# Attention with two MoE-like layers on one core: the first layer's chunks beside the attention go from two of 288 tokens a batch in every step to one of 512 in every second step

## The chip, the cores and the metric

The kernel runs on one core of one Trainium2 chip. The metric is the device time of one execution in microseconds (us): the median of the runs before is 996.87 us (three runs, 996.81 to 996.87). TensorE is called PE, VectorE DVE, ScalarE ACT, GpSimd POOL, SyncE SP, as in the profile.

## The reference: what is computed

Inputs are in fp32; q, k, v are (4 batches, 8 heads, 576 positions, 64), s is (4, 8, 576).

```python
scores = scale * np.matmul(q, k.transpose(0, 1, 3, 2))
cum = np.cumsum(np.maximum(s, 0.0), axis=-1)
bias = -(cum[:, :, :, None] - cum[:, :, None, :])
scores = np.where(causal, -1000000000.0, scores + np.minimum(bias, 0.0))
scores = scores - np.max(scores, axis=-1, keepdims=True)
attn = np.exp(scores)
attn = attn / (np.sum(attn, axis=-1, keepdims=True) + 1e-09)
x = np.matmul(attn, v)                      # then (4 * 576 tokens, 512)
h = x @ w_in;  x = np.maximum(0.01 * h, h) @ w_out                                   # layer 0
h = x @ w2_in; x = (np.maximum(h, 0) + np.log1p(np.exp(-np.abs(h)))) @ w2_out        # layer 1
```

Both layers have 2304 tokens, 512 channels and 2048 hidden channels. The weights come in as double precision; the kernel splits each fp32 operand into a high and a low part, and takes three matmuls (high x high, high x low, low x high) for each product.

## The kernel before, in words

**The two stages.** Stage one is the attention, up to some 267 us; stage two is the rest of the two layers, in eight groups: layer 0 and 1, four groups of four blocks of 128 hidden channels each. The order of the instructions on every engine is the order in which the program records them (a manual schedule); a small clock (`later`, `tick`, L64 to L77) records a follow-up so many ticks later.

**The attention** (L154 to L467) takes two heads at a time, a pair p, 16 pairs in all. A pair has four steps, i = 0 to 3 (`order`, L419): the 512-wide last full block of rows, the 64 left-over rows of both heads (288 columns a piece), the 384-wide block, and the two first blocks together (256 + 128). Step n = 4p + i goes from 0 to 66, and has two ticks. Work on one step's tile goes through the engines over four steps. In step n, in this order, PE makes the scores of tile n+1 (L273, L283); DVE the minima of tile n (`maxima`, L302; for the left-over rows a last tiny combination, L307); ACT the exponentials of tile n (L316); DVE the divisors and POOL the normalisation of tile n-1 (L322, L323, L327); PE the transposes of tile n-2 into PSUM (L335, L339, L344), first half, then second half; ACT and DVE their copies to SBUF (L356, L358). In steps i = 0 and i = 2 PE ends with the product with V of the pair before (`pv`, L375), whose result ACT and DVE split into `xh` and `xl` (L382, L386).

**The fill units** (class `Fill`, L470 to L565). Between the first and the second transposes of each step, `fill.step(n)` (L491) puts in one unit of layer 0's first group (four hidden blocks) for a batch that is through the attention. An h unit (L530) is 12 matmuls for one hidden block; ACT, ACT again and POOL then make `gf`, `gh` and `gl` one tick after the other (L537, L542, L547). An o unit (L552) is 12 matmuls for one block of 128 output channels; ACT copies it to `o` (L562), and SP stores it to DRAM (`part`, L563). `ready(b)` (L519) lists the units of batch b once its last `xl` is there: two chunks of CW = S // 2 = 288 tokens, eight units each. `run` (L510) takes the first unit of the list if its weights and operands are recorded, else none. Weights are loaded and split by tables of steps (L480 to L482); the fourth output block is split in step 25, so that no o unit can be recorded ahead of step 28. Units that are left at the end are taken after the attention (L577).

**Stage two** starts with the first group for batch 3, as two chunks of 288 tokens (`first`, L596), then takes the other seven groups in five chunks (512, 512, 256, 512, 512). One step is one hidden block of one chunk: 12 matmuls of `h_mm` (L143), and three steps later the 12 matmuls of `out_mm` (L676). Partial sums of the fill units come back from `part` into `acc` by six loads (`load_acc`, L586, planned at L707).

**SBUF.** The split weights lie in `wpool` (L84), eight buffers for each of four tags, taken at the start.

Of the kernel before, what the change touches and what calls it, by code (L numbers as in the profile page):

```python
# [9 lines left out]
F32 = mybir.dt.float32  # L10
I32 = mybir.dt.int32
U32 = mybir.dt.uint32
F32R = mybir.dt.float32r
# [4 lines left out]
P = 128  # L18
NEG = -8.0e9
G = 4  # L20
# [10 lines left out]
def attn_moe_moe(ctx, tc, q, k, v, s, w1i, w1o, w2i, w2o, out):  # L31
    nc = tc.nc

    B, H, S = s.shape
    D = v.shape[-1]
    NT, DM = out.shape
    DFF = w1i.shape[1]
    KD = DM // P
    NF = DFF // P
    NG = NF // G  # L40
    NPAIR = H // 2
    NP = B * NPAIR
    NB = S // P
    TL = S - NB * P
    CW = S // 2
    scale = 1.0 / float(D) ** 0.5

    nc.scalar.preload_act_table_set("natural_log_exp_and_others")
# [1 line left out]
    def pool(name, bufs=1, **kw):  # L50
        return tc.tile_pool(name=name, bufs=bufs, **kw)

    dram = ctx.enter_context(pool("dram", space=bass.MemoryType.DRAM))
# [4 lines left out]
    xh = keep.tile([P, KD, NT], F32R, tag="xh", name="xh")  # L58
    xl = keep.tile([P, KD, NT], F32R, tag="xl", name="xl")
    bb_d = dram.tile([B * H, 2, S], F32R, tag="bb_d", name="bb_d")  # L60
    part = dram.tile([2 * B, P, KD, CW], F32, tag="part", name="part")


    todo = {}  # L64
# [2 lines left out]
    def later(n, fn, *args):  # L67
        todo.setdefault(clock[0] + n, []).append((fn, args))
# [12 lines left out]


    wt, wio = {}, {}
    wpool = ctx.enter_context(pool("wpool", bufs=2 * G))  # L84
    wio["tmp"] = ctx.enter_context(pool("wtmp", bufs=2))

    def load_w(layer, f, nm, place=None):
        w = ((w1i, w1o), (w2i, w2o))[layer]["io".index(nm)].bitcast(I32)
        raw = (place or wio[nm]).tile([P, 2 * DM], I32, tag="raw", name="raw" + nm)
        if nm == "i":  # L90
            nc.sync.dma_start(
                raw.rearrange("p (k f) -> p k f", k=KD),
                w[:, 2 * f * P:2 * (f + 1) * P].rearrange("(k p) f -> p k f", p=P),
            )
        else:
            nc.sync.dma_start(raw, w[f * P:(f + 1) * P, :])
        wt[layer, f, nm, "raw"] = raw.rearrange("p (e t) -> p e t", t=2)

    def split_w(layer, f, nm, at):

        raw = wt.pop((layer, f, nm, "raw"))
        L, Hw = raw[:, :, 0], raw[:, :, 1]
        m = wio["tmp"].tile([P, DM], I32, tag="wm", name="wm")
        t = wio["tmp"].tile([P, DM], I32, tag="wt", name="wt")
        nc.scalar.activation(m.bitcast(F32), Hw.bitcast(F32), AF.Abs)
        nc.scalar.activation(t, L.bitcast(U32), AF.Copy, scale=2.0 ** -29)

        mf = m.bitcast(F32)

        def clamp():  # L110
            nc.vector.tensor_scalar(mf, mf, D_MIN, D_MAX, op0=ALU.max, op1=ALU.min)

        def shift():
            nc.vector.tensor_scalar(m, m, 3, 0x3FFFFFFF, op0=ALU.logical_shift_left, op1=ALU.bitwise_and)

        def sign():
            nc.vector.scalar_tensor_tensor(m, Hw, -0x40000000, m, op0=ALU.bitwise_and, op1=ALU.bitwise_or)  # L117

        def add():
            nc.gpsimd.tensor_tensor(m, m, t, op=ALU.add)  # L120

        def high():
            hi = wpool.tile([P, DM], F32R, tag=f"w{nm}h", name=f"w{nm}h")
            nc.scalar.activation(hi, m.bitcast(F32), AF.Copy)
            wt[layer, f, nm] = [hi]

        def low():
            lo = wpool.tile([P, DM], F32R, tag=f"w{nm}l", name=f"w{nm}l")
            hi = wt[layer, f, nm][0]
            nc.gpsimd.tensor_tensor(lo, m.bitcast(F32), hi.bitcast(F32), op=ALU.subtract)  # L130
            wt[layer, f, nm].append(lo)

        for n, fn in zip(at, (clamp, shift, sign, add, high, low)):
            later(n, fn)


    def h_mm(ps, layer, f, xh, xl):
        hi, lo = wt[layer, f, "i"]
        n = 0
        for kk in range(KD):  # L140
            w = slice(kk * P, (kk + 1) * P)
            for a, b in ((hi[:, w], xh[:, kk, :]), (hi[:, w], xl[:, kk, :]), (lo[:, w], xh[:, kk, :])):
                nc.tensor.matmul(ps, a, b, start=n == 0, stop=n == 3 * KD - 1)  # L143
                n += 1
# [325 lines left out]
    class Fill:  # L470
# [20 lines left out]
        def step(self, n):  # L491
            if n == 4 * NPAIR + 1:
                self.begin()
            if n in self.loads:
                (f, nm), place = self.loads[n]
                load_w(0, f, nm, wio[place])
            if n in self.splits:
                split_w(0, *self.splits[n][0], (1, 2, 3, 4, 5, 6))
            self.run()

        def bank(self, nm):

            tag, bufs = ("m", 1) if not self.free else self.free.pop(0)
            if self.free is not None:
                self.free.append((tag, bufs))
            return self.ps.tile([P, 512], F32, tag=tag, name=nm, bufs=bufs)[:, :CW]

        free = None

# [7 lines left out]
                fn(*args)  # L517

        def ready(self, b):  # L519
            hs, os = [], []  # L520
            for ch in range(2):
                c0 = b * S + ch * CW
                x = xh[:, :, c0:c0 + CW], xl[:, :, c0:c0 + CW]
                gs = {}
                hs += [(self.h, (f, x, gs)) for f in range(G)]
                os += [(self.o, (dm, 2 * b + ch, gs)) for dm in range(KD)]

            self.units += hs[:G + 1] + os[:KD] + hs[G + 1:] + os[KD:]

        def h(self, f, x, gs):  # L530
            ps = self.bank("ps_h")
            h_mm(ps, 0, f, *x)
            new = lambda pool, nm, dt=F32: pool.tile([P, CW], dt, tag=nm, name=nm)

            def leaky():
                gf = new(self.tpool, "gf")
                nc.scalar.activation(gf, ps, AF.Prelu, alpha=0.01)  # L537
                later(1, high, gf)

            def high(gf):  # L540
                gh = new(self.gpool, "gh", F32R)
                nc.scalar.activation(gh, gf, AF.Copy)  # L542
                later(1, low, gf, gh)

            def low(gf, gh):
                gl = new(self.gpool, "gl", F32R)
                nc.gpsimd.tensor_tensor(gl, gf, gh.bitcast(F32), op=ALU.subtract)  # L547
                gs[f] = gh, gl

            later(1, leaky)  # L550

        def o(self, dm, c, gs):  # L552
            ps = self.bank("ps_o")
            w = slice(dm * P, (dm + 1) * P)
            for f in range(G):
                (wh, wl), (gh, gl) = wt[0, f, "o"], gs[f]
                for n, (a, b) in enumerate(((wh, gh), (wh, gl), (wl, gh))):
                    nc.tensor.matmul(ps, a[:, w], b, start=f == 0 and n == 0, stop=f == G - 1 and n == 2)  # L558

            def store():  # L560
                o = self.tpool.tile([P, CW], F32, tag="o", name="o")
                nc.scalar.activation(o, ps, AF.Copy)  # L562
                nc.sync.dma_start(part[c, :, dm, :], o)  # L563

            later(1, store)  # L565

    with pool("psA", bufs=2, space=PSUM) as psA:
# [11 lines left out]
            tick()  # L579
        fill.stack.close()  # L580

    for nm in "io":
        wio[nm] = ctx.enter_context(pool("raw" + nm))
    acc = ctx.enter_context(pool("accpool")).tile([P, KD, NT], F32, tag="acc", name="acc")

    def load_acc(c):  # L586
        nc.sync.dma_start(acc[:, :, c * CW:(c + 1) * CW], part[c])


    gpool = ctx.enter_context(pool("gpool", bufs=4, side="right"))  # L590
# [2 lines left out]
    ps_o = ctx.enter_context(pool("ps_o", bufs=5, space=PSUM))  # L593

    chunks = [(0, 512), (512, 512), (1024, NT - 2048), (NT - 1024, 512), (NT - 512, 512)]
    first = [((B - 1) * S + ch * CW, CW) for ch in range(2)]  # L596
    groups = [(layer, g) for layer in range(2) for g in range(NG)]
    steps = []
    for layer, g in groups:
# [17 lines left out]
    gs = {}  # L617
# [80 lines left out]
    for gi, (layer, g) in enumerate(groups[1:]):  # L698
        a, z = start[groups[gi]], start[layer, g]
        when = [(a + n - 1, a + n) for n in (0, 3, 6, 8, 11, 14, 16, 19)] if gi else [None] * 4 + [(0, 2), (1, 4), (3, 6), (5, 8)]  # L700
        for j, at in enumerate(when):
            if at:
                f, nm = divmod(j, 2)
                w = (layer, g * G + f, "io"[nm])
                plan.setdefault(at[0], []).append((load_w, w))
                plan.setdefault(at[1], []).append((split_w, (*w, (1, 1, 1, 1, 2, 2))))
    for c in range(2 * (B - 1)):  # L707
        plan.setdefault(2 * c + 2, []).append((load_acc, (c,)))

    for n, (layer, g, c, is_first, is_last, f) in enumerate(steps):  # L710
# [63 lines left out]
```

## Time and profile before

| | us |
|---|---|
| median of three runs | 996.87 |
| the profiled execution's own time | 996.93 |
| its span, first to last instruction | 995.1 |
| PE busy | 974.9 (98%) |
| POOL, ACT, DVE busy | 569.7, 539.3, 529.6 |

The profiled execution is 0.06 us above the median, and 1.8 us of its time lie outside the span. Busy shares are means over the whole span: the attention stage is read from its own stretches, by the chain of waits (what ended last, step by step) and by busy times in stretches of about one pair.

### The profile page before, as it was taken

The numbers are of one execution on the slowest core, as the hardware profiler recorded it, in microseconds if no ns is written. First come the engines' busy times: TensorE is split into PE (matmuls) and PEld (weight loads), VectorE is DVE, ScalarE is ACT, GpSimd is POOL, SyncE is SP. The second block draws the span as 40 slices with busy tenths as digits, with TensorE's granted clock in tenths as the row PEclk, the third lists the DMA queues.
The fourth block names the chain that finished last, engine by engine and source line by source line (L and its number), as shares of the span: only waits on it lengthen the run. The fifth ranks groups of instructions, "written<-read, shape, count | busy, mean of one in ns | idle before, by whom it ended". The sixth has DMA issues, their size and how long they took to land.

```text
span 995.1 us, 15228 instructions
## 1 busy us (share of the span) xinstructions
PE 974.9 (98%) x5498; PEld 810.7 (81%) x5498; DVE 529.6 (53%) x1139; ACT 539.3 (54%) x1153; POOL 569.7 (57%) x564
## 2 busy tenths in 40 slices
PE   7889999999999999999999999999999999999998
PEld 4567788888898888888888888888888888888886
DVE  7787556554222332132215447767687868763534
ACT  5777666666454333334334546676657655654452
POOL 6657455534256444444444446777867786775553
PEclk9999999999999999999999999999999999999999
DMA  5422333221153111111111111111111111100202
GB/s 176 140 84 80 104 112 115 64 74 44 37 197 128 43 43 43 43 43 43 45 41 43 43 42 43 43 43 43 43 43 43 43 42 43 43 1 1 85 22 85
DMA packets 38411, 62.04 MB, mean 62 GB/s; under 512 B 2790, under 2 KB 25830, under 8 KB 38336
## 3 DMA queue, kind: packets, MB, share of 16 engines
q1 hardware_dynamic: 38192, 60.74, 18.7%
q8 instruction: 44, 0.72, 0.3%
q10 hardware_dynamic: 144, 0.33, 0.1%
q14 instruction: 31, 0.25, 0.1%
HBM read 52.65 MB, written 8.40 MB: 61 GB/s over the span
## 4 chain that ended last, share of the span: by engine, by line
PE 92%; DVE 3%; ACT 3%; POOL 1%; issue 1%; ACTq 0%; POOLq 0%
PE ps_h L143 40%; PE ps_out L676 36%; PE pt_v L375 4%; PE pt_s L283 4%; PE ps_o L558 3%; PE pt_t L344 3%; PE pt_s L273 2%; ACT sc L316 1%; DVE sc L302 1%; PE pt_t L339 1%; DVE st L307 0%; ACT PA L356 0%; DVE wm L117 0%; ACT xh L382 0%; DVE acc L686 0%
## 5 line engine op out<-in xcount | busy, mean ns | idle before, releaser
L150 POOL TENSOR_TENSOR gl<-gf,gh 128x512 fp32r<-128x512 f32 (+2 forms) x148 | 181.2, 1225 | 138.6 <-ACT gh L149 128.9
L143 PE MATMUL ps_h<-xh,wih 128*128 128x512 f32 (+2 forms) x688 | 245.8, 357 | 0.6 <-ACT o L562 0.6
L143 PE MATMUL ps_h<-xl,wih 128*128 128x512 f32 (+2 forms) x688 | 243.8, 354 | 0.0
L143 PE MATMUL ps_h<-xh,wil 128*128 128x512 f32 (+2 forms) x688 | 243.7, 354 | 0.0
L686 DVE TENSOR_TENSOR acc<-ps_out,acc 128x512 f32<-128x512 f32 (+1 forms) x114 | 73.7, 662 | 164.4 <-PE ps_out L676 164.4
L641 POOL TENSOR_TENSOR t<-e,t 128x512 f32<-128x512 f32 (+1 forms) x80 | 112.4, 1405 | 72.0 <-DVE t L640 71.3
L327 POOL TENSOR_SCALAR sc<-sc,st 128x512 f32<-128x512 f32 (+4 forms) x160 | 87.6, 559 | 109.1 <-DVE st L323 65.5
L143 PEld LDWEIGHTS ps_h<-xh,wih 128*128 128x128 f32 x688 | 129.5, 188 | 19.1 <-ACT o L562 0.8
L143 PEld LDWEIGHTS ps_h<-xl,wih 128*128 128x128 f32 x688 | 129.6, 188 | 18.0
L143 PEld LDWEIGHTS ps_h<-xh,wil 128*128 128x128 f32 x688 | 129.5, 188 | 17.6
L625 ACT ACTIVATE gf<-ps_h 128x512 f32<-128x512 f32 (+2 forms) x68 | 36.6, 538 | 170.2 <-PE ps_h L143 170.0
L676 PE MATMUL ps_out<-woh,gl 128*128 128x512 f32 x288 | 112.3, 390 | 0.0
L676 PE MATMUL ps_out<-woh,gh 128*128 128x512 f32 x288 | 112.3, 390 | 0.0
L676 PE MATMUL ps_out<-wol,gh 128*128 128x512 f32 x288 | 112.2, 390 | 0.0
L149 ACT ACTIVATE gh<-gf 128x512 fp32r<-128x512 f32 (+2 forms) x148 | 85.4, 577 | 49.3 <-DVE gf L651 48.6
L316 ACT ACTIVATE sc<-sc,st 128x512 f32<-128x512 f32 (+2 forms) x144 | 83.5, 582 | 39.2 <-DVE st L307 19.7
L120 POOL TENSOR_TENSOR wm<-wm,wt 128x512 int32<-128x512 int32 x64 | 85.0, 1330 | 31.3 <-DVE wm L117 31.3
L302 DVE CUSTOM_DVE_ANT_0 sc<-pt_s,mask 128x512 f32<-128x512 f32 (+2 forms) x144 | 66.8, 480 | 59.5 <-PE pt_t L344 48.3
L676 PE MATMUL ps_out<-gh,wol 128*128 128x512 f32 (+2 forms) x272 | 97.8, 360 | 0.0
L676 PE MATMUL ps_out<-gh,woh 128*128 128x512 f32 (+2 forms) x272 | 97.7, 359 | 0.0
L676 PE MATMUL ps_out<-gl,woh 128*128 128x512 f32 (+2 forms) x272 | 97.7, 359 | 0.0
L640 DVE TENSOR_SCALAR t<-e 128x512 f32<-128x512 f32 (+1 forms) x80 | 44.3, 554 | 98.1 <-ACT e L631 98.1
(102 smaller groups left out, 1732.7 us busy)
## 6 DMA issues: line engine op xcount, KB each, us to landing
rawi<-in_moe_w_in SPq DMA_DIRECT2D x32, 512.0 KB
rawo<-in_moe_w_out SPq DMA_DIRECT2D x32, 512.0 KB
V<-in_v SPq DMA_DIRECT2D x16, 320.0 KB
Q<-in_q SPq DMA_DIRECT2D x15, 320.0 KB
K<-in_k SPq DMA_DIRECT2D x16, 288.0 KB
out<-acc SPq DMA_DIRECT2D x18, 256.0 KB
part<-o SPq DMA_DIRECT2D x24, 144.0 KB
acc<-part SPq DMA_DIRECT2D x6, 576.0 KB
```

What stands on the lines that cost most here:

```text
L120: nc.gpsimd.tensor_tensor(m, m, t, op=ALU.add)
L143: nc.tensor.matmul(ps, a, b, start=n == 0, stop=n == 3 * KD - 1)
L149: nc.scalar.activation(gh, gf, AF.Copy)
L150: nc.gpsimd.tensor_tensor(gl, gf, gh.bitcast(F32), op=ALU.subtract)
L283: nc.tensor.matmul(self.ps[j][:, c], x[r, t * P:(t + 1) * P], y[r, :(t + 1) * P], start=x is Q[i], stop=x is bq,)
L302: nc.vector.tensor_tensor_reduce(out=self.sc[:, j, c], in0=self.ps[j][:, c], in1=m, scale=-scale, scalar=3.0e38, op0=ALU.add, op1=ALU.min, ...
L316: nc.scalar.activation(x, x, AF.Exp, scale=-1.0, bias=self.stat(0, e), accum_out=self.stat(1, e))
L327: nc.gpsimd.tensor_scalar(x, x, self.stat(2, e), 1.0, op0=ALU.mult, op1=ALU.mult)
L640: nc.vector.tensor_scalar(t, e, 1.0, -1.0, op0=ALU.add, op1=ALU.add)
L641: nc.gpsimd.tensor_tensor(t, e, t, op=ALU.subtract)
L676: nc.tensor.matmul(ps, a, b, start=f == 0 and m == 0, stop=f == G - 1 and m == 2)
L686: nc.vector.tensor_tensor(d, o, d, op=ALU.add)
```

## The change

Layer 0's first group now takes one chunk of FW = 512 tokens for each of batches 0 to 2 beside the attention: tokens 0 to 511 with batch 0, 512 to 1023 with batch 1, 1024 to 1535 with batch 2. The other 768 tokens come first in stage two, as two chunks of 384. A fill unit is begun in even steps alone (i = 0 and i = 2), and in every step after 64. There are 24 units in place of 48. The weights' pool becomes one of six buffers, taken at the start, and one of two, taken after the attention; `part` comes back by three loads of 1 MB in place of six of 576 KB.

```diff
-    CW = S // 2
+    FW = 512
...
-    part = dram.tile([2 * B, P, KD, CW], F32, tag="part", name="part")
+    part = dram.tile([B - 1, P, KD, FW], F32, tag="part", name="part")
...
-    wpool = ctx.enter_context(pool("wpool", bufs=2 * G))
+    wpools = [ctx.enter_context(pool("wpool0", bufs=6))]
...
+        wp = wpools[(layer * NF + f) % (2 * G) // 6]
...
-            self.run()
+            if n % 2 == 0 or n > 4 * NP:
+                self.run()
...
         def ready(self, b):
-            hs, os = [], []
-            for ch in range(2):
-                c0 = b * S + ch * CW
-                x = xh[:, :, c0:c0 + CW], xl[:, :, c0:c0 + CW]
-                gs = {}
-                hs += [(self.h, (f, x, gs)) for f in range(G)]
-                os += [(self.o, (dm, 2 * b + ch, gs)) for dm in range(KD)]
-
-            self.units += hs[:G + 1] + os[:KD] + hs[G + 1:] + os[KD:]
+            c, gs = slice(b * FW, (b + 1) * FW), {}
+            x = xh[:, :, c], xl[:, :, c]
+            self.units += [(self.h, (f, x, gs)) for f in range(G)] + [(self.o, (dm, b, gs)) for dm in range(KD)]
...
+    wpools.append(ctx.enter_context(pool("wpool1", bufs=2)))
...
-        nc.sync.dma_start(acc[:, :, c * CW:(c + 1) * CW], part[c])
+        nc.sync.dma_start(acc[:, :, c * FW:(c + 1) * FW], part[c])
...
-    first = [((B - 1) * S + ch * CW, CW) for ch in range(2)]
+    n0 = (B - 1) * FW
+    n1 = (NT - n0) // 2
+    first = [(n0, n1), (n0 + n1, n1)]
...
-    for c in range(2 * (B - 1)):
+    for c in range(B - 1):
         plan.setdefault(2 * c + 2, []).append((load_acc, (c,)))
```

**POOL, between two pairs in the attention, h units in the list.** `sc` rows are normalisations (512 wide belongs to i = 0, 288 to i = 1, 384 to i = 2, 256 and 128 to i = 3), `gl` the last part of an h unit. Before:

```order
L547 TENSOR_TENSOR gl<-gf,gh 128x288
L327 TENSOR_SCALAR sc<-sc,st 128x512 x2
L547 TENSOR_TENSOR gl<-gf,gh 128x288
L327 TENSOR_SCALAR sc<-sc,st 128x288 x2
L547 TENSOR_TENSOR gl<-gf,gh 128x288
L327 TENSOR_SCALAR sc<-sc,st 128x384 x2
```

Now:

```order
L328 TENSOR_SCALAR sc<-sc,st 128x256
L328 TENSOR_SCALAR sc<-sc,st 128x128
L328 TENSOR_SCALAR sc<-sc,st 128x512 x2
L543 TENSOR_TENSOR gl<-gf,gh 128x512
L328 TENSOR_SCALAR sc<-sc,st 128x288 x2
L328 TENSOR_SCALAR sc<-sc,st 128x384 x2
L543 TENSOR_TENSOR gl<-gf,gh 128x512
```

A `gl` now stands behind the normalisations of two steps out of four, and is 512 wide.

**ACT, from the `xh` of step i = 0 to the `xh` of step i = 2.** `sc` are exponentials, PB and PA copies of transposes, `gf` and `gh` the parts of an h unit. Before:

```order
L382 ACTIVATE xh<-pt_v 128x192
L316 ACTIVATE sc,st<-sc,st 128x576
L356 ACTIVATE PB<-pt_t 128x3x128
L537 ACTIVATE gf<-ps_h 128x288
L316 ACTIVATE sc,st<-sc,st 128x384
L542 ACTIVATE gh<-gf 128x288
L316 ACTIVATE sc,st<-sc,st 128x384
L356 ACTIVATE PA<-pt_t 128x4x128
L537 ACTIVATE gf<-ps_h 128x288
L382 ACTIVATE xh<-pt_v 128x384
```

Now:

```order
L383 ACTIVATE xh<-pt_v 128x192
L538 ACTIVATE gh<-gf 128x512
L317 ACTIVATE sc,st<-sc,st 128x576
L357 ACTIVATE PB<-pt_t 128x3x128
L317 ACTIVATE sc,st<-sc,st 128x384 x2
L357 ACTIVATE PA<-pt_t 128x4x128
L533 ACTIVATE gf<-ps_h 128x512
L383 ACTIVATE xh<-pt_v 128x384
```

The `gh` of the even step's unit stands between `xh` and the left-over rows' exponential, and step i = 1 has no `gf` of its own.

**PE, the end of the attention.** `pt_t` are transposes, `pt_v` the last product with V. Before:

```order
L375 MATMUL pt_v<-PB,V_93 64x128 x2
L375 MATMUL pt_v<-PB,V_93 64x256 x4
L375 MATMUL pt_v<-PB,V_93 64x128 x2
L558 MATMUL ps_o<-gh,woh 128x288
L558 MATMUL ps_o<-gl,woh 128x288
L558 MATMUL ps_o<-gh,wol 128x288
```

Now:

```order
L345 MATMUL pt_t<-ident,sc 128x128 x6
L376 MATMUL pt_v<-PB,V_93 64x128 x2
L376 MATMUL pt_v<-PB,V_93 64x256 x4
L376 MATMUL pt_v<-PB,V_93 64x128 x2
L144 MATMUL ps_h<-xh,wih 128x384
L144 MATMUL ps_h<-xl,wih 128x384
```

No unit is left behind the last product with V; stage two's first matmul follows it at once.

## Rows read from the trace of the kernel before

**Rows 1.** The page: its span, and PE's busy time.
```profile
span 995.1 us, 15228 instructions
PE 974.9 (98%) x5498; PEld 810.7 (81%) x5498; DVE 529.6 (53%) x1139; ACT 539.3 (54%) x1153; POOL 569.7 (57%) x564
```

**Rows 2.** PE's waits from 270 us on: engine, line, releaser, total us, times, longest.
```profile
PE ps_h L143 <- ACT o L562: 0.6, 1, 0.6
```

**Rows 3.** Stretches of one pair: PE, PEld, DVE, ACT, POOL busy, granted clock, DMA.
```profile
28.20:41.20 13.00, 11.22 (x92) 7.86 (x92) 10.31 (x39) 9.52 (x28) 8.47 (x12) 1.00 0.35 116
...
117.80:135.00 17.20, 17.20 (x143) 14.33 (x141) 9.59 (x38) 11.84 (x33) 10.08 (x15) 1.00 0.29 96
```

**Rows 4.** The chain of waits in order of time, 117 to 137 us: start, us, what.
```profile
117.89 1.29 PE pt_s L283 x6
119.18 0.59 PE pt_t L339 x4
...
126.52 1.02 PE pt_s L283 x6
...
128.01 1.59 PE ps_h L143 x12
...
130.97 0.59 PE pt_t L344 x4
...
133.59 1.48 PE pt_v L375 x16
135.09 0.49 ACT xh L382
...
136.99 0.30 PE pt_t L335
```

**Rows 5.** The same view at five other places of stage one and stage two.
```profile
69.97 1.29 PE pt_s L283 x6
...
242.08 1.56 PE pt_v L375 x20
...
275.39 6.59 PE ps_h L143 x48
281.98 1.58 PE ps_out L676 x12
...
296.28 2.76 PE ps_h L143 x12
...
312.07 2.72 PE ps_out L676 x12
...
336.56 1.43 PE ps_h L143 x12
```

**Rows 6.** Instructions in order of time on POOL, DVE and ACT around 243 us.
```profile
243.18 1.36 POOL L327 TENSOR_SCALAR sc<-sc,st 128x512 f32<-128x512 f32 x2 [0.83 <-DVE st L323]
244.50 0.80 POOL L547 TENSOR_TENSOR gl<-gf,gh 128x288 fp32r<-128x288 f32 x1
...
243.92 0.43 ACT L542 ACTIVATE gh<-gf 128x288 fp32r<-128x288 f32 x1
245.35 0.78 ACT L316 ACTIVATE sc<-sc,st 128x576 f32<-128x576 f32 x1 [0.99 <-DVE st L307]
...
246.13 0.47 ACT L356 ACTIVATE PB<-pt_t 128x384 f32<-128x384 f32 x1
...
244.82 0.49 DVE L307 TENSOR_TENSOR st<-st 128x1 f32<-128x1 f32 x1
```

**Rows 7.** The same view at 79, 227 and 268 us, on POOL and DVE.
```profile
79.16 1.29 POOL L130 TENSOR_TENSOR wol<-wm,woh 128x512 fp32r<-128x512 f32 x1
...
79.75 0.71 DVE L307 TENSOR_TENSOR st<-st 128x1 f32<-128x1 f32 x1
...
227.72 0.16 DVE L307 TENSOR_TENSOR st<-st 128x1 f32<-128x1 f32 x1
...
268.29 0.56 DVE L386 TENSOR_TENSOR xl<-pt_v,xh 128x384 fp32r<-128x384 f32 x1 [4.62 <-ACT xh L382]
```

More of the change, by code (lines that the diff above doesn't have):

```diff
@@ L122, in high @@
         def high():
-            hi = wpool.tile([P, DM], F32R, tag=f"w{nm}h", name=f"w{nm}h")
+            hi = wp.tile([P, DM], F32R, tag=f"w{nm}h", name=f"w{nm}h")
             nc.scalar.activation(hi, m.bitcast(F32), AF.Copy)
@@ L127, in low @@
         def low():
-            lo = wpool.tile([P, DM], F32R, tag=f"w{nm}l", name=f"w{nm}l")
+            lo = wp.tile([P, DM], F32R, tag=f"w{nm}l", name=f"w{nm}l")
             hi = wt[layer, f, nm][0]
@@ L505, in bank @@
                 self.free.append((tag, bufs))
-            return self.ps.tile([P, 512], F32, tag=tag, name=nm, bufs=bufs)[:, :CW]
+            return self.ps.tile([P, 512], F32, tag=tag, name=nm, bufs=bufs)
         free = None
@@ L532, in h @@
             h_mm(ps, 0, f, *x)
-            new = lambda pool, nm, dt=F32: pool.tile([P, CW], dt, tag=nm, name=nm)
+            new = lambda pool, nm, dt=F32: pool.tile([P, FW], dt, tag=nm, name=nm)
             def leaky():
@@ L560, in store @@
             def store():
-                o = self.tpool.tile([P, CW], F32, tag="o", name="o")
+                o = self.tpool.tile([P, FW], F32, tag="o", name="o")
                 nc.scalar.activation(o, ps, AF.Copy)
```

## The prediction, made before the changed kernel ran

> **What bounds the kernel now.** First the page: PE is busy for 974.9 of 995.1 us [rows 1]. That is a mean over two unlike stages, so I looked next at PE's waits by stretch: from 270 us to the end PE waited 0.6 us in all [rows 2]. Stage two is therefore PE's own work, and a change there is worth what it does to the number and width of matmuls. For stage one I compared the busy times of two pairs [rows 3]. A pair without fill units took 13.00 us, with PE busy for 11.22 and no engine full: there the handing on from engine to engine sets the pace. A pair with four units took 17.20 us, and PE was busy for all of it. The chain of waits of that same pair is nearly all PE [rows 4]. So the units fill what the attention leaves of PE and then some, and with them stage one too is bound by PE. The granted clock is 1.00 in both stretches, so 2.4 GHz throughout, even where PE waited for 1.8 us in 13: I charge nothing for the clock.
>
> **Prices of PE's work.** From the start of the pair at 117.89 to the end of its last product with V at 133.59 + 1.48 = 135.07 are 17.18 us [rows 4]. Four units lie in them, at 1.58 to 1.60 each (one is shown, 1.59), so the pair's own work is 17.18 - 6.37 = 10.81 us. Twelve matmuls of 512 columns take 2.72 us and of 256 columns 1.43 us [rows 5]; that is 226.7 and 119.2 ns a matmul, against 132 ns for 288 columns. For 384 columns no row exists; halfway between 256 and 512 lies 172.9 ns, 2.07 us for twelve.
>
> **The change, part by part.**
>
> *The units.* 48 units of 1.59 (76.3 us) become 24 of 2.72 (65.3 us): 11.0 us less.
>
> *The first group of stage two.* Eight steps are sixteen twelves of matmuls, 16 x 1.58 = 25.3 us before [rows 5] and 16 x 2.07 = 33.1 us now: 7.8 us more. Together PE's work falls by 3.2 us, since the columns are the same and 288 matmuls with their fixed part go. The Trainium skill, TensorE: Matmul & The Clock Gate, "Back-to-back issue gap", gives a warm gap of N / 2.4 + 2.5 ns, so 122.5 ns for 288 and 215.8 for 512 columns. By that rule the same count saves only 0.7 us. The rows say 132 and 226.7, so I keep 3.2 and leave the rule's case to the rivals.
>
> *Waits of PE before.* From the start of step 19 at 69.97 to stage two's first matmul at 275.39 are 205.4 us [rows 5]. The units take 76.3. The attention's own work is eleven pairs of 10.81, less 1.3 for scores that step 63 no longer has to make, plus 2.0 for step 19 and about 4.5 for the last three steps: 124.1. So PE waited for 5.0 us. Some of that goes: steps 24 to 27 had no unit, since the o units' weights come only in step 28, and now steps 24 and 26 have their h units.
>
> *Waits of PE after: the light steps.* Units now lie in i = 0 and i = 2 alone, which have the product with V already, so PE's work per step is some 6.2, 1.8, 6.2 and 2.0 us. In the light ones PE runs ahead, and meets two chains.
> After i = 2: the product with V ends at 135.07, ACT makes `xh`, two exponentials and a copy, and PE's transpose at L335 begins at 136.99 [rows 4]. In this pair that step happened to have no unit. PE's own way there is 1.29 + 0.59 = 1.88, the chain took 1.92: a wait of 0.05, twelve times, 0.6 us.
> After i = 0: PE's own way from the end of the product with V to the transposes of step i = 2 is 4.45 less the unit of 1.59, 2.86 us [rows 4]. Counted from the end of the transposes at 242.08, that is 1.56 + 2.86 = 4.42 [rows 5]. The other way there goes `xh`, `xl`, the minima, the tiny L307, the left-over rows' exponential and the copy PB. L307 is asked for at 244.82, 2.74 after 242.08 [rows 6]. From its end to the transposes are 0.04, 0.78 and 0.47 us and the signal, 1.34 [rows 6]. L307 alone takes 0.16 [rows 7], which makes 2.74 + 0.16 + 1.34 = 4.24: in time, by 0.2. But L307 does not end while POOL is within an instruction: at 244.82 it lasted till 245.31, when `gl` ended (244.50 + 0.80) [rows 6], and at 79.75 it lasted 0.71, till POOL's 1.29 us were over [rows 7]. Now `gl` is 512 wide; the nearest row for that is the 512-wide 1.29. Its `gh` starts at 1.84 as here (243.92) and takes 0.6 to 0.7 (between the 0.43 for 288 and the 0.78 for 576 columns), so `gl` begins at about 2.55, just ahead of L307, and ends at 3.85. PE can go on at 3.85 + 1.34 = 5.2: a wait of 0.8. This happens in i = 0 steps with an h unit, two for each of three batches. In the first two of these a weight split's instruction is between the normalisations, as at 79.16, and lets L307 through between two of POOL's instructions; there I take 0.3. Together 4 x 0.8 + 2 x 0.3 = 3.8 us. Its bounds are 0 (if `gl` starts after L307) and 12 x 0.8 (if something of POOL's holds it in every pair).
>
> *The end of stage one.* The units of batch 2 are all begun by step 64, so that nothing covers the last tile. The last product with V waits for the second copy, 0.65 us by a copy like PB's 0.47 and its signals (bounds 0.5 and 0.8), and stage two's first matmul waits for `xh` and `xl`, 0.02 + 0.49 + 0.56 and a signal, 1.13 [rows 4, 6, 7]. 1.8 us.
>
> *What costs nothing.* ACT, DVE and POOL have less to do for the units (12 `gf`, `gh`, `gl`, 12 `o`, each 512 wide, in place of 24 of 288); only their place matters, and that is counted above. On SP, twelve stores and three loads of `part` move the same bytes less a ninth; the loads stand behind the same weight loads, and `acc` of the first chunk is needed in step 14 of stage two, some 40 us after its load. If this cover failed, DVE's additions would stop PE for a transfer, a few us. The later buffers of the weights' pool lie where the attention's tiles were, free before their first use.
>
> *The sum.* Waits after are 3.8 + 0.6 + 1.8 = 6.2 against 5.0, 1.2 us more; work is 3.2 us less. The profiled execution took 996.93 (0.06 over the median), so 996.93 - 2.0 = 994.9; rounding with the median, **994.8 us**, 0.2% faster. About 0.2% (2.0 us) is also what a measurement of this kernel can tell from no change, so the forecast stands on the edge of being told.
>
> **The rivals.**
>
> *B, L307 goes free.* If `gh` takes so long, or DVE so little, that `gl` starts after L307, the four long waits go: 994.8 - 3.2 = 991.6. The margin is only about 0.2 us. Against it: in the rows `gl` held L307 also where both began within 0.3 us of each other. The Trainium skill, SBUF — State Buffer, "Who interferes with whom", says a DVE instruction with two SBUF inputs and a GpSimd one exclude each other for the whole of whichever began first. By that rule, a `gl` that comes second would wait for 0.16 and no more.
>
> *C, the light steps wait as an unfed pair does: slower.* The pair without units took 13.00 for 10.81 of work, 2.2 us of waits [rows 3]. Half of the steps now have no unit; if they keep half of that wait, 1.1 us a pair, twelve pairs wait 13.2 in place of 3.8 + 0.6: 994.8 + 8.8 = 1003.6. It decides for slower from 0.7 us a pair. For it: both chains above are as long as PE's way, to a tenth. Against: in the unfed pair weight splits lie on ACT and DVE in every step, and a heavy step of 6.2 us lets the other engines catch up.
>
> *D, held in the o pairs too.* With an o unit, the normalisations end at 244.54, 0.28 ahead of L307 [rows 6]. If they begin 0.3 later, the second of them holds L307 by up to 0.35 more than the slack, six times: 994.8 + 2.1 = 996.9, no change.
>
> *E, width saves little.* If a matmul's cost went by its columns alone, 512 columns would take 2.83 a unit and 384 2.12 a twelve: 994.8 + 24 x 0.11 + 16 x 0.05 = 998.2, still within 0.2%. The rows of both widths speak against it. The skill's gap rule would give 994.8 + 2.5 = 997.3.
>
> That the change does not do what it says is excluded by the order: all 24 units stand ahead of the last product with V.
>
> **How the numbers follow.** Forecast 0.46, B 0.16, C 0.18, D 0.17, E 0.03. The forecast's own spread is some 1 us, so half of its chance lies on either side of 2.0 us. Faster by over 0.2%: 0.23 + 0.16 = 0.39, with a little of D, 0.41. Within 0.2%: 0.23, D and E, 0.41. Slower: C, 0.18. The range goes from B with some room, 991.0, up to 999.0, through D and E and the start of C, and leaves out most of C.
>
> **What would show it.** Units of 2.72 us and twelves of 2.07 us on PE; pairs of 16.3 us with o units and 17.1 with h units; L307 lasting about 1.1 us after an h unit in i = 0 and 0.16 after an o unit; stage two's first matmul near 265.5 us and its step 8 near 292.5 (before: 296.28). Wrong: pairs of over 17.2 us, PE waiting for normalisations or scores in light steps, L307 short throughout, or any wait of PE for `acc`.

## The result and the profile after

The changed kernel takes **1002.14 us** (median of 6 runs, 1002.12 to 1002.16) against 996.84 (6 runs, 996.73 to 996.88): ratio 1.0053, 95% interval 1.0043 to 1.0064. It is slower by 5.3 us; the forecast was 994.8, 0.2% faster, and the range ended at 999.0.

Lines of the changed kernel are numbered one higher than before here: L308 is the L307 of the prediction, L336, L345 and L357 are the transposes' and copies' lines, L543 is `gl`, L554 the o unit. The pairs below are counted p0 to p15 as the loop runs over them; batch 1 is p4 to p7, and its units lie in p9 to p12. A pair whose units are h units is called an h pair, one with o units an o pair: p9 and p10 are h pairs, p11 and p12 o pairs. The time of a pair is taken from the start of its scores at L274 to the next pair's.

The page of the changed kernel, to lay beside [rows 1]:

```profile
span 1000.3 us, 14549 instructions
PE 974.0 (97%) x5210; PEld 795.4 (80%) x5210; DVE 530.7 (53%) x1139; ACT 534.5 (53%) x1117; POOL 568.1 (57%) x552
```

PE is busy for as long as before (974.0 against 974.9) though it has 288 instructions less, and the span is 5.2 us longer. So PE waits more. The chain of waits in order of time says from where on (start, us, what):

```profile
272.30 8.62 PE ps_h L144 x48
...
317.00 2.72 PE ps_out L675 x12
```

Stage two's first matmul comes at 272.30, where 265.5 was forecast. From there to 317.00, where the first group is over and both programs do the same, are 44.70 us, against 312.07 - 275.39 = 36.68 before [rows 5]: 8.0 more, 7.8 forecast. The list of PE's waits has nothing behind that point. All of the miss but half a microsecond lies in stage one. The longest of PE's waits there, from 60 to 275 us (total, times, longest):

```profile
PE pt_t L345 <- ACT PB L357: 5.2, 6, 1.2
PE pt_t L336 <- ACT PA L357: 1.9, 2, 1.4
PE ps_h L144 <- DVE xl L387: 1.2, 1, 1.2
PE pt_v L376 <- ACT PB L357: 0.5, 1, 0.5
```

Two pairs of batch 1, the first with h units and the first with o units (the columns are those of [rows 3]):

```profile
140.35:157.83 17.48, 16.52 (x116) 12.31 (x116) 10.80 (x39) 11.34 (x31) 9.21 (x13) 1.00 0.27 90
175.31:191.86 16.55, 16.48 (x117) 12.31 (x116) 9.25 (x38) 11.23 (x32) 7.69 (x12) 1.00 0.26 85
```

The pair of [rows 3] was full at 17.20. These have less work and are not full. The four h pairs of batches 1 and 2 (p9, p10, p13, p14) take 17.47 or 17.48 us each, the o pairs 16.55 to 16.86. What stands in the chain of such an h pair:

```profile
147.74 1.10 DVE st L308
...
148.93 0.87 ACT sc L317 x2
149.80 0.38 ACT PB L357
...
150.31 0.63 PE pt_t L345 x4
150.94 2.75 PE ps_h L144 x12
...
154.13 1.48 PE pt_v L376 x16
...
155.63 0.49 ACT xh L383
156.12 0.87 ACT sc L317 x4
156.99 0.49 ACT PA L357
...
157.53 0.30 PE pt_t L336
```

At two places the chain leaves PE. From 145 to 150.3 us, in the step without a unit behind i = 0, the way goes over L308, the exponential and the copy PB. From 155.6 to 157.5, behind i = 2, it goes over `xh`, two exponentials and the copy PA. At the first, POOL and DVE one under the other:

```profile
147.56 1.26 POOL L543 TENSOR_TENSOR gl<-gf,gh 128x512 fp32r<-128x512 f32 x1
...
147.74 1.09 DVE L308 TENSOR_TENSOR st<-st 128x1 f32<-128x1 f32 x1
```

L308 is asked for 0.18 us after `gl` began, and ends when `gl` ends (147.56 + 1.26 = 148.82). That is the lock that the prediction had drawn from [rows 6]. L308 lasts 1.08 to 1.10 us in the four h pairs and 0.16 to 0.27 in the o pairs.

**A part of the 5.3 us has nothing to do with units.** The whole attention is already 1 us late at the first pair:

```profile
4.99 0.83 DVE L187 TENSOR_SCALAR sc<-sc 128x576 f32<-128x576 f32 x1 [2.00 <-DMA sc<-in_s]
...
15.40 0.16 DVE L308 TENSOR_TENSOR st<-st 128x1 f32<-128x1 f32 x1
```

In the kernel before these two start at 4.61 (for 0.53 us) and 14.33. The first of them reads the two rows of `s` and starts some 0.4 us later; it then runs beside POOL's clearing of `BQ`, and so do the next copies (1.15 us for the two at L214, where 0.62 stood), until 1.07 us are lost. That these last longer because of POOL is read from the overlap and was not tested by itself.

### The profile page after: what moved, and what is told of

It reads as the page before. It is cut to its first block, busy times and chain, and to the rows that moved or that the text cites. A ratio compares the mean times of both kernels' runs of the same rounds, so it can differ in the third digit from the quotient of the medians.

```text
span 1000.3 us, 14549 instructions
## 1 busy us (share of the span) xinstructions
PE 974.0 (97%) x5210; PEld 795.4 (80%) x5210; DVE 530.7 (53%) x1139; ACT 534.5 (53%) x1117; POOL 568.1 (57%) x552
## 4 chain that ended last, share of the span: by engine, by line
PE 88%; ACT 6%; DVE 4%; issue 1%; POOL 0%; DMA 0%; ACTq 0%; DVEq 0%; POOLq 0%
PE ps_h L144 39%; PE ps_out L675 36%; PE pt_v L376 4%; PE ps_o L554 3%; PE pt_t L345 3%; ACT sc L317 2%; PE pt_s L284 1%; PE pt_s L274 1%; DVE sc L303 1%; DVE st L308 1%; ACT xh L383 1%; ACT PA L357 1%; DVE wm L118 0%; DVE xl L387 0%; ACT wt L107 0%
## 5 line engine op out<-in xcount | busy, mean ns | idle before, releaser
L144 PE MATMUL ps_h<-xh,wih 128*128 128x512 f32 (+2 forms) x640 | 236.7, 370 | 1.2 <-DVE xl L387 1.2
L144 PE MATMUL ps_h<-xl,wih 128*128 128x512 f32 (+2 forms) x640 | 235.6, 368 | 0.0
L144 PE MATMUL ps_h<-xh,wil 128*128 128x512 f32 (+2 forms) x640 | 235.6, 368 | 0.0
L144 PEld LDWEIGHTS ps_h<-xh,wih 128*128 128x128 f32 x640 | 120.6, 188 | 21.0 <-DVE xl L387 1.4
L144 PEld LDWEIGHTS ps_h<-xl,wih 128*128 128x128 f32 x640 | 120.6, 188 | 19.5
L144 PEld LDWEIGHTS ps_h<-xh,wil 128*128 128x128 f32 x640 | 120.5, 188 | 19.6
```

## The experiments

Theory at the start: the miss is the sum of the late start, of the lock in a step that has no unit to cover it, and of a small wait behind i = 2 in every pair. Rivals: the lock is the whole of it; any step without a unit costs the same; or a 512-wide unit costs by itself, wherever it is put. Ratios are to the kernel before on the same chip (medians of 996.76 to 996.87).

### The pools of six and two alone

The kernel before with this edit:

```diff
-    wpool = ctx.enter_context(pool("wpool", bufs=2 * G))
+    wpools = [ctx.enter_context(pool("wpool0", bufs=6))]
...
+        wp = wpools[(layer * NF + f) % (2 * G) // 6]
...
+    wpools.append(ctx.enter_context(pool("wpool1", bufs=2)))
```

> The kernel before with the weights' pools of six and two and nothing else of the change. The changed kernel's first L308 starts at 15.40 us and the kernel before's at 14.33, with the same program up to there; the small landing of s in sc came 0.4 us later. Theory one, the pools' new places in memory bring the late start: first combination near 15.4 and 997.9 us. Theory two, the start belongs to the other edits' places in memory or in the program: 14.3 us and 996.8, within 0.2. Rival: six and two buffers hold up a split of weights and the time rises by over 1.5 us.

996.89 us, ratio 1.0001 (0.9992 to 1.0011); the first L308 at 14.4 us in the profiled execution. Theory two holds: the pools cost nothing and do not make the start late. But one of its ten executions took 997.85, and the others 996.74 to 997.02. So the start seems to be early or late by execution, with about 1 us between, and a kernel only makes the one or the other likely. The kernel before has the late value in few executions (997.88 once among the 25 taken beside these).

### `gl` a tick later

```diff
-                later(1, low, gf, gh)
+                later(2, low, gf, gh)
```

> The changed kernel with each h unit's gl one tick later, behind the pair's L308 in program order. Lock theory: the four h steps of i = 0 in batches one and two hold L308 for 1.1 us where it takes 0.16 to 0.3 elsewhere; with gl later they fall to 0.3 or less, the four h pairs from 17.47 to about 16.6, and the kernel from 1002.1 to about 998.6. Rival one, the lock moves to the next small operation of VectorE: pairs of 17.2 or more, 1001 to 1002. Rival two, the 512 wide h unit costs the pair by itself (ScalarE's and GpSimd's longer operations), not by L308: L308 short and the pairs still 17.4, 1002.

1001.61 us, ratio 1.0049 (1.0032 to 1.0066), its profiled execution with an early start 1000.59. The time moved by half a microsecond, yet L308 is short in every pair from p7 on. The three pairs behind one another (two h, one o):

```profile
140.24:156.82 16.58, 16.52 (x116) 12.32 (x116) 9.87 (x39) 11.35 (x31) 9.11 (x13) 1.00 0.29 93
156.82:173.87 17.05, 16.54 (x117) 12.34 (x116) 10.40 (x39) 11.32 (x31) 9.50 (x14) 1.00 0.30 93
173.87:191.82 17.95, 16.77 (x117) 12.24 (x117) 8.95 (x38) 11.24 (x31) 7.71 (x13) 1.00 0.24 78
```

The h pairs did gain 0.90 and 0.43 (in the second a split of weights stands in the chain in place of `gl`). The first o pair lost 1.4, for its unit now waited for the last `gl`:

```profile
PE ps_o L554 <- POOL gl L543: 2.2, 2, 1.1
```

The edit had taken one wait away and made another, which neither theory had foreseen. It decides nothing about the total; a later kernel repeats it without the fault.

### Units in the odd steps

```diff
-            if n % 2 == 0 or n > 4 * NP:
+            if n % 2 == 1 or n > 4 * NP:
```

> The changed kernel with a unit begun in every odd step (i = 1 and 3) and not in every even one. Lock theory: no gl of an h unit stands near L308 any more, h pairs and o pairs alike; with the light step after i = 2 (wait 0.23 each pair) now filled: 16.4 to 16.6 us a pair, 997.5 to 998.5 in all with the late start, 1 less without it. Rival, any step without a unit waits, wherever it is, since i = 0 and 2 now have none: pairs of 17 or more, 1001 to 1004.

995.61 us, ratio 0.9987 (0.9978 to 0.9997). Nine of ten executions, the profiled one among them, have the late start; one took 994.52. Only the parity differs from the change, and 6.5 us go. Two pairs of batch 1, the first with two h units (p9) and the last with two o units (p12):

```profile
139.46:155.88 16.42, 16.42 (x117) 12.30 (x116) 9.99 (x38) 11.32 (x30) 9.17 (x13) 1.00 0.48 147
188.86:205.30 16.44, 16.44 (x118) 12.31 (x117) 9.67 (x35) 9.91 (x27) 7.60 (x12) 1.00 0.28 92
```

PE is full, and h and o pairs are alike (16.43 to 16.54 from p8 on). Stage two begins at 265.84 with the late start. No `gl` stands near L308 any more, but in p8 and p12 L308 lasts 1.00 and 1.08 us beside a split's instruction on POOL (`wm`, 127.70 to 128.98, and `wol`, 193.85 to 195.16). These pairs take 16.44 and 16.43 all the same: step i = 1 has a unit here. So neither the width of a unit nor its absence from half of the steps costs much by itself; it matters from which steps it is absent. The steps i = 0 and i = 2 have the product with V and, with units on both sides, cover their chains without one. The expected 997.5 to 998.5 was too high by 2, mostly since the way from p15's scores to stage two fell as well, from 29.0 us (272.30 - 243.26) to 27.7.

### Units in halves

```diff
+        rest = None
+
+        def run(self, first=True):
+            if self.rest:
+                fn, self.rest = self.rest, None
+                fn()
+            elif self.units and first:
...
-            h_mm(ps, 0, f, *x)
+            h_mm(ps, 0, f, *x, ks=(0, 1))
...
+            def second():
+                h_mm(ps, 0, f, *x, ks=(2, 3))
+                later(1, leaky)
+
+            self.rest = second
```

(The first half of a unit in even steps, the second in odd ones; o units likewise by f.)

> The changed kernel with each unit's twelve matmuls in two halves of six, the first in even steps and the second in odd ones, so no step is without a unit's matmuls and gl comes at the place of the odd units. Theory of the lock and the light steps: pairs of 16.35 us as their own work of 10.81 + 5.5 goes, PE's waits in stage one back to the 5 us of the kernel before, 996.0 with the late start and 995.0 without. Lock alone (light steps cost nothing): the same as with odd units. Rival, width (512 wide evictions and stores on ScalarE and GpSimd) costs whatever the pacing: pairs of 16.8 or more, 999 to 1002.

994.74 us, ratio 0.9979 (0.9969 to 0.9988). Nine executions lie at 994.69 to 994.85 and one, the profiled one with an early start, at 993.70. The pairs take 16.32 to 16.35 us, their own work of 10.81 + 5.5, but for p7 and p11, which have one unit instead of two (14.2). The forecast of the theory (995.0 and 996.0) was 1.3 too high. It had PE wait for 5 us in stage one; from step 19 at 69.86 to stage two at 263.97 are 194.1 us, and 66.2 for units and 124.1 of own work leave 3.8.

### Halves that end in even steps

The same with the parity of the halves turned, so that `gl` comes just ahead of L308 again, but the step behind has six matmuls of a unit.

> The halved units, but the first half in odd steps and the second in even ones, so gl of the units that end in i = 0 comes again just ahead of L308, with no step left without a unit's matmuls. Theory, the lock costs only because step i = 1 is light and shows it on PE: L308 of 1.1 us in four pairs as in the changed kernel, pairs still 16.3 to 16.6, 993.7 to 995.2 with the early start. Rival, the lock costs its 0.9 whatever PE has to do: pairs of 17.2 in four, 997.0 to 998.5.

The lock is there, in the instructions of POOL and DVE in order of time:

```profile
160.02 1.30 POOL L547 TENSOR_TENSOR gl<-gf,gh 128x512 fp32r<-128x512 f32 x1
...
160.21 1.12 DVE L308 TENSOR_TENSOR st<-st 128x1 f32<-128x1 f32 x1
```

and PE does not feel it in that pair (columns of [rows 3]):

```profile
154.02:170.35 16.33, 16.33 (x118) 12.26 (x117) 10.63 (x38) 11.35 (x32) 9.15 (x14) 1.00 0.29 95
```

For the pairs the theory holds to a few hundredths: the lock costs nothing where the step has other work. The total does not: 998.50 us (996.85 to 999.73, in three clusters), ratio 1.0017 (1.0008 to 1.0026). That lies in the rival's range, but not for the rival's reason, since no pair takes 17.2. From p15's scores to stage two are 34.8 us here for 66 matmuls of units still to be done, and 32.9 for 72 in the halves before. In that tail the turned order makes PE's transposes wait for `gl` and for PA, which they do not do in the tail of the halves before:

```profile
PE pt_t L336 <- ACT PA L357: 1.4, 1, 1.4
PE pt_t L345 <- POOL gl L547: 0.9, 1, 0.9
```

Behind these waits the granted clock of TensorE fell, in the profiled execution (998.40), from 1.00 to 0.50, so from 2.4 to 1.2 GHz, and rose again 3.41 us later. From 247.01 to 250.79, just before, PE had been busy for 1.39 of 3.78 us. The stretch at the lower clock (columns of [rows 3]), and the chain in it:

```profile
251.80:255.21 3.41, 3.41 (x20) 2.60 (x17) 0.47 (x2) 0.33 (x1) 1.02 (x3) 0.50 0.00 0
```

```profile
251.31 2.47 PE pt_v L376 x20
253.78 2.27 PE ps_o L564 x6
```

At the full clock such a product takes 1.56 us (at 237.31) and six matmuls of a unit 1.39 (at 256.38), so the fall cost 1.8 us. It goes with the three clusters: the mean granted clock is 0.999 to 1.000 in the executions near 996.9, 0.997 to 0.998 near 998.4 and 0.996 near 999.7. A second such fall would fit the slowest ones, but only one of the middle was profiled. What is left above the theory at the full clock, 996.86 against 995.2 and 1.05 more for the late start, may be the waits of the tail; no run takes these away.

### `gl` later for two of four units

```diff
-                later(1, low, gf, gh)
+                later(2 - f % 2, low, gf, gh)
```

> The changed kernel with gl one tick later for the units of f = 0 and 2 alone, which begin in i = 0, so the last gl is as early as in the change and the first o unit does not wait for it. Lock theory with light steps: the pairs with L308 short go from 17.48 to 16.6 and, where a split of weights (wm) stands in the chain in its place, to 17.05; o pairs stay at 16.6; 2.7 us less in batches one and two, so 999.4 with the late start and 998.4 without. Rival, the lock is all of the h pairs' loss: 16.55 in all four, 998.5 and 997.5. Rival, light steps alone and no lock: h pairs stay over 17.2, 1001 or more.

998.92 us, ratio 1.0022 (1.0012 to 1.0031), with a late start: 3.2 less than the change. L308 lasts 0.16 in all four h pairs, no o unit waits for `gl`, and the pairs are 16.58, 17.06 and 16.58 (h, h, o of batch 1), 16.58 and 16.57 (h of batch 2). The pairs are as expected, but for the second h pair of batch 2, where no split stood in the chain any more. So the lock is worth 0.90 us in three pairs and 0.42 in p10, where a split takes its place: 3.1 of the 3.2 us. In the pairs, 16.58 remain where 16.34 are work.

### The tiny rows first

On the halves, the two rows of `s` ahead of K's first pair:

```diff
-            load(0, "k")
             load(0, "q", nc.scalar)
...
+            load(0, "k")
             nc.sync.dma_start(c0, s.rearrange("b h s -> (b h) s"))
```

> The halves with the two tiny rows of s loaded ahead of K's first pair on SP. Of the runs so far the late start (1.05 us) was in all of the change's, 9 of 10 of the odd units and of the halves, and 1 of 10 with the pools alone. Theory, the rows land late behind K's 288 KB: with them first the start is early in every execution, 993.7 and no second value 1.05 us up. Rival, what lands late is not behind K: values stay split, most near 994.75, or K itself is late and all are slower.

993.54 us, ratio 0.9966 (0.9953 to 0.9979), 993.07 to 993.66 in five executions: early in all, by their times. The rows are issued at 1.33 us in either order; what moves is K's pair, from 0.72 to 2.08.

On the change alone, the same edit:

> The changed kernel with the two tiny rows of s ahead of K's first pair on SP and nothing else. Theory, the late start is a matter of what these rows are queued behind and is apart from the units: most executions start early (14.3 to 14.4 us for the first L308) and take 1001.1, pairs unchanged at 16.6 and 17.48. Rival, in this program it is late wherever the rows stand: 1002.1.

1001.27 us, ratio 1.0046 (1.0029 to 1.0063): 1001.10 to 1001.30 in three executions and 1002.38 in one. The profiled one:

```profile
4.21 0.46 DVE L187 TENSOR_SCALAR sc<-sc 128x576 f32<-128x576 f32 x1 [1.23 <-POOL ident masks.py:197]
...
14.25 0.16 DVE L308 TENSOR_TENSOR st<-st 128x1 f32<-128x1 f32 x1
```

The h pairs stay at 17.51, the o pairs at 16.6. The start is 0.9 to 1.0 us of the miss and apart from the units. The edit makes the late start rare, not impossible: two of the fourteen executions with the rows first have it, one here and one in the next kernel. What makes it likely in the changed program is open.

### An o unit let in by two of its four `gl`

On the halves with the rows first:

```diff
-                if fn == self.o and len(args[2]) < G or any(len(wt.get((0, f, nm), ())) < 2 for f in fs):
+                if fn == self.o and len(args[2]) < 2 or any(len(wt.get((0, f, nm), ())) < 2 for f in fs):
```

> The same with an o unit's first half let in as soon as two of the four gl are there, as it needs no more. In the halves pairs seven and twelve are 14.2 us and not 16.3: both slots of a unit stay empty there, and two units go to the tail, which takes 32.9 us after the last block's scores. Theory, work put off to the tail is done there with waits of 3 to 4 us between: with no slot lost 1 to 2 us less than h_start, near 992.5. Rival, the tail is bound by its own chain and not by the units: the same time within 0.3; second rival, the second half waits for the last gl, 1.1 us in each batch: 994 to 995.

992.61 us, ratio 0.9958 (0.9944 to 0.9972): the fastest, 4.2 us under the kernel before. Four executions took 992.30 to 992.84; the profiled one took 993.88 and has a late start. (The pairs that the expectation calls seven and twelve are p7 and p11.) No slot is empty and every pair from p5 to p14 takes 16.32 to 16.35. The reason is not quite the expected one, waits in the tail. Two units less lie in the tail, and it is 5.2 us shorter, about their work. An empty slot had shortened its pair by 2.1 us (14.23), not by the unit's 2.77, so each of the two units put off had cost about 0.7.

### Units in steps 1 and 2, and in steps 3 and 0

```diff
-            if n % 2 == 0 or n > 4 * NP:
+            if n % 4 in (1, 2) or n > 4 * NP:
```

and `(0, 3)` in the other.

> The changed kernel with units begun in steps i = 1 and 2; steps 3 and 0 have none. Theory, the step i = 3 without a unit costs 0.24 us a pair by the chain of the copy xh, the exponentials and the copy PA, and the step i = 1 without one costs 0.9 in a pair whose L308 is held: here only the first is left, 16.6 us for o and h pairs alike, 997.5 to 999.0. Rival, any two steps without a unit cost the same as the change's: 16.6 and 17.48, 1001 to 1002. Rival, all of it comes from a unit in an even step: 16.9 to 17.1.

> The changed kernel with units begun in steps i = 3 and 0; steps 1 and 2 have none. Theory as for the units in steps 1 and 2: step 3 is filled, so o pairs go to 16.35 to 16.45; the h unit begun in i = 0 still puts its gl ahead of L308, and step 1 has nothing to cover it, so h pairs keep 17.2 to 17.3; 999.5 to 1001.0. Rival, step 3 is what counts and the lock is covered: 16.4 in all pairs, 996 to 998.

Units in 3 and 0: 999.29 us, ratio 1.0022 (1.0013 to 1.0032). The pairs come out as the theory said, to a few hundredths: 17.31, 17.29 and 17.28 us where an h unit lies in i = 0 and L308 lasts 1.09 to 1.11 (p9, p10, p14), 16.32 to 16.43 in p7, p8, p12 and p13. With step 3 filled the o pairs have lost their 0.2, with step 1 empty the lock costs its 0.9. The total is 0.2 under the expected range. One of each:

```profile
139.23:156.54 17.31, 16.40 (x118) 12.31 (x117) 10.93 (x38) 11.35 (x30) 9.20 (x13) 1.00 0.44 140
204.47:220.84 16.37, 16.37 (x118) 12.31 (x117) 8.21 (x35) 9.29 (x26) 5.14 (x10) 1.00 0.41 132
```

Units in 1 and 2: 1007.54 us, ratio 1.0103 (1.0088 to 1.0118), the slowest of all, where 997.5 to 999.0 was expected and the rivals gave at most 1002. Its four executions lie at 1005.78, 1006.72, 1008.37 and 1008.39. In the profiled one, the last, the granted clock was 0.50 again, 1.2 GHz, for 3.41 us from 265.83, after PE had been busy for 1.39 of the 3.47 us from 261.72 to 265.19; a product with V and a unit in it take 2.84 and 3.30 us in place of 1.57 and 2.77, 1.8 us more. Of the four only the two at 1008.4 have a mean clock of 0.998. The rest is in the pairs: L308 lasts 0.16 in p9 to p11, p13 and p14, and yet these take 16.75 to 17.29. The chain of waits from the end of p9 into p10:

```profile
157.03 1.48 PE pt_v L376 x16
...
158.52 0.49 ACT xh L383
159.01 0.87 ACT sc L317 x4
159.88 0.48 ACT PA L357
160.37 0.52 ACT gh L538
160.89 0.89 ACT sc L317 x4
...
162.49 0.18 DVE PZ L359
...
162.80 0.52 PE pt_t L345 x3
163.32 1.57 PE pt_v L376 x20
```

With steps 3 and 0 both empty, the chain behind i = 2 is not caught up in i = 0 but runs on, over the next exponentials and the copy PZ, for which the next product with V waits. Where the copy `gh` of an h unit of the pair before stands in that chain, as here, a pair loses 0.95 us (p10, p11, p14); p9 and p13, which follow an o pair, lose 0.42. In the change, steps 1 and 3 are empty and an o pair loses 0.2; with the odd units it is steps 0 and 2, and 0.1; with units in 3 and 0 it is steps 1 and 2, also two in a row, and at most 0.1 where L308 is not held. The prices of empty steps do not add: it depends on which chain the empty steps leave open.

## Why the prediction was wrong, step by step

Its account of stage one ran from the scores at 69.97 to stage two's first matmul, 205.4 us, as units 76.3, own work 124.1 and waits 5.0 [rows 5]. The same stretch is now 272.30 - 70.92 = 201.4: units 24 x 2.76 = 66.2, own work 124.1, waits 11.1. The forecast had 6.2 for these waits.

- **The start** was not in the sum at all: it is 0.95 late at 70.92, and the rows of `s` put first show that it is apart from the units. The prediction had taken the program up to there as unchanged.
- **A unit of 512 columns** takes 2.75 to 2.77 us beside the attention, not 2.72: 24 x 0.04 = 0.9. The rows had been read in stage two. **Twelves of 384** take 2.08 as forecast (2.07). By the Trainium skill's gap rule (TensorE: Matmul & The Clock Gate, "Back-to-back issue gap") 512 columns would take an estimated 215.8 ns; the runs have 230 (2.76 / 12), and the measurement decides.
- **L308 held by `gl`** was right in place and cause. Forecast was 4 x 0.8 + 2 x 0.3 = 3.8. Measured at this place are 4 x 0.9 in the four h pairs and 0.5 in p6: 4.1. Not all of that is the lock: moving `gl` gave back 3.1, since in p10 a split takes its place; in p6 ACT's split ends later (98.03) than L308 (97.75), and in p5 L308 is short (0.28). Rival B, that it goes free, fell: `gl` began 0.18 us ahead of L308. The Trainium skill's rule that issue order decides who blocks (SBUF — State Buffer, "Who interferes with whom") agrees with the trace, 147.56 ahead of 147.74.
- **The wait behind i = 2**, "a wait of 0.05, twelve times, 0.6 us", is the first **step that failed**. Measured are 0.23 in each of the pairs p4 to p14, 2.5 us in all. The row was there: the transpose at 136.99 stands with 0.30 in the chain [rows 4], and one that follows a unit without a wait adds 0.11 to it. I had counted to its start. From the end of the product with V to the scores behind it were 2.22 us for 1.29 + 0.59 + 0.11 = 1.99 of work. The idle time itself is 0.07, near the forecast; what I had left out is that behind a wait the transpose no longer overlaps the matmul ahead of it. The error was 0.2, eleven times. Another 0.3 was lost in p7 alone, where the first o unit's last matmul waited 0.44 for POOL's split (`wol`).
- **The end of stage one**: 1.8 was forecast, about 3.8 measured (28.9 us from 243.42 to 272.30, less 11.0 for four units and 14.0 of own work), and this is the other **step that failed**. The last `xl` waits as forecast (1.17), and for the last PB PE is idle for 0.46, forecast 0.65. The step that I had not followed is the one ahead of them: at 257.79 the last pair's i = 2 ends, and PE's next transposes wait for PA from there to 260.19, with 0.7 us of work in between:

```profile
257.80 0.50 ACT xh L383
...
258.33 0.56 DVE xl L387
...
259.44 0.61 DVE PA L359
...
260.19 0.52 PE pt_t L345 x3
260.71 2.77 PE ps_o L554 x12
```

In the last steps no pair follows whose scores would fill that light step, so the same chain that costs 0.23 elsewhere costs 1.7 there. The remaining 0.4 lies in two pieces of PE's own that were longer than elsewhere, the last unit (2.96 for 2.76) and the last product (1.72 for 1.48).

Together these are the start 0.95, the units 0.9, the place of L308 0.3, behind i = 2 and in p7 2.2, the tail 2.0, and 0.5 in stage two: 6.9 of the 7.3 us between 994.8 and 1002.14.

Rival C had the sign and nearly the time, 1003.6, and it put the cause in the light steps, which the parity shows to be right: 6.5 us between even and odd. That its time came so near is in part luck, for 0.95 of the 1002.14 is the start, which it did not have. Its mechanism was too even. It gave 1.1 us to every pair; the o pairs lost 0.2 to 0.5 and the h pairs 1.14. My argument against it, that a heavy step lets the others catch up, holds for steps i = 0 and i = 2 without a unit (odd units, pairs of 16.44). It does not hold for i = 1 and i = 3, which are light already and have now lost their units. I weighed whether light steps wait, and had both chains as long as PE's way to a tenth. An error of 0.2 in something that happens eleven times was then as large as the gain that was forecast.

Rival D fell (L308 lasts 0.16 to 0.27 with o units), and so did E beyond the 0.9 above.

The saving itself is real: half as many units at 512 columns are 10.1 us less in stage one for 8.0 more in the first group. The change gave it back by where it put them, and the late start came on top.

## What to carry to other kernels

When work is made coarser, ask of each step that loses its share which chain it had covered, and put the coarse pieces into the steps whose own work is least; here the same 24 units cost 6.5 us more in the steps that were already heavy. Better still, cut a piece in two where it is issued and keep its width, so that every step keeps some. Where a chain and the work that covers it are equal to a tenth, read the row behind the wait to its end and multiply by the number of times before calling it free.

## What the hardware showed that I had not expected

- A PE instruction behind a short wait costs more than the wait, though it is hardly longer itself. The transpose behind i = 2, first in the kernel before, where it follows a unit without a wait, then in the change, behind a wait of 0.07 us:

```profile
121.19 0.27 PE L335 MATMUL pt_t<-ident,sc 128*64 128x128 f32 x1
```

```profile
157.53 0.30 PE L336 MATMUL pt_t<-ident,sc 128*64 128x128 f32 x1
```

Without a wait it overlaps the matmul ahead of it and adds 0.11 to the chain; behind one it adds its whole 0.30. In the o pairs of the change this is nearly the whole loss: PE is busy for 16.48 of 16.55 us, with 16.34 of work. Four transposes in a row show little of it: at L345 they add 0.63 behind a wait (150.31) and 0.59 at the same place without one (184.40).
- A few hundredths at the start decide 1 us of the whole run. The first reader of the two rows of `s`, L187 here, starts at 4.61 to 4.75 us in the four profiled executions with K's pair ahead and an early start, and takes 0.46 to 0.53. In the seven with a late start it starts at 4.83 to 5.19 and ends at 5.82 or 5.83 in every one. POOL's first clearing of `BQ` begins at 4.87 to 4.89 in all of these. The copies behind it are then late too (7.37 and not 6.70) and longer (1.15 and not 0.62), and nothing makes it up later. That fits two values of the time and no spread between them; that POOL's clearing is what holds the reader was not tested.
- In the profiled executions of two kernels the granted clock fell to 1.2 GHz for 3.41 us, each time in the tail and after PE had mostly waited, and cost 1.8 us. In both kernels the slower executions are those with the lower mean clock. The change itself shows no such fall.
